# Batch 0 of a windowed attention and GEGLU kernel: v requested before the second run of q and k, the run's transposes placed behind the products with v

## Chip, cores, metric

One core of one Trainium2 chip. The metric is device time in microseconds (us). One execution that was traced gives the profile; each kernel was also run several times, and runs of the kernel before were taken on the same chip beside it. One run of the kernel before took 589 us; it is left out of everything below.

## The reference

```python
# q, k, v: (8 batches, 8 heads, 576 positions, 64)
scores = scale * q @ k^T + alibi bias;  mask: 0 <= i - j < 128
attn = softmax(scores);  o = attn @ v
x = o as (4608 tokens, 512)
out = (gelu(x @ w_gate) * (x @ w_val)) @ w_out      # d_ff = 1536
```

Operands on the chip are bf16, the output is f32.

## The kernel before

The kernel is one long stream of matmuls: attention of a batch runs ahead of the feed-forward part that uses it. The opening cannot do that: batch 0 needs its data first. Its first 320 positions (q and k as a "first run", five positions to a partition) are transposed, scored, exponentiated and masked, summed, multiplied with v, scaled into xT; then the first gate and value products start. The other 256 positions ("second run") are needed only for the scores after that. The stretch with the order before:

```python
load_runs(0, 0, 4, 8)            # first run, heads 4 to 7 (0 to 3 came earlier)
load_runs(0, 1, 0, 8)            # second run of q and k (kept in vb[1])
load_v(0, (0, 1, 2))
load_w(0, 256)
load_w(256, 640)
...
def rest(cs):                    # transposes of the second run, two head pairs at a time
    for w in (0, 1):             # q, k
        ps = bank().bitcast(BF16)
        for k, c in enumerate(cs):
            transpose_runs(0, 1, w, c, ps[:, 256 * k:256 * k + 256])
        untangle(act, 0, 1, w, slice(cs[0], cs[-1] + 1), ps)
...
keep_busy(8)                     # matmuls on zeros ahead of the next bank's first use
first((0, 1))                    # has keep_busy(3) between q and k
made_later()
keep_busy(4)
scores(0, 0, (0, 1), lambda: (keep_busy(3), first((2,)), first((3,))))
keep_busy(2)
scores(0, 0, (2, 3))
scores2(0)
keep_busy(4)
rest((0, 1))
keep_busy(1)
rest((2, 3))
sums0(0)
...
values_first((act, dve, act, dve))   # products with v, spread of 1/sum, scaling into xT
scores(0, 1, (0, 1), None, masks)
...                                  # gate_val: first gate and value products
```

`keep_busy(n)` puts n matmuls of 128x512 on zeros ahead of the next use of a PSUM bank, so that TensorE does not idle. In what follows these are "fillers".

The softmax here doesn't subtract the row's maximum and nothing guards it: scores larger than these inputs give would overflow.

Of the kernel before, what the change touches and what calls it, by code (L numbers as in the profile page):

```python
# [26 lines left out]
def kernel(  # L27
# [39 lines left out]
    def bank():  # L67
        ps = psum.tile([128, 512], FP32, name="ps")
        for _ in range(heat.pop()):
            nc.tensor.matmul(out=ps, lhsT=zeros[:, 0:128], rhs=zeros, start=True, stop=True)  # L70
        heat.append(0)
        return ps

    def keep_busy(n):
        heat[0] = n
# [20 lines left out]
    def load(t, src, b, js=range(5)):  # L96
        for j in js:
            lo = 64 if j == 0 else 0
            nc.gpsimd.dma_start(  # L99
                out=t[lo:128, j, :].rearrange("p (h d) -> p h d", h=H),  # L100
                in_=src[b][:, 128 * j - 64 + lo:128 * j + 64, :].rearrange("h p d -> p h d"))
# [10 lines left out]
    def runs(what, b, n):  # L112
        first, parts, r = RUNS[b][n]
        t, lo, p = (qs, ks)[what][b], 1536 * n, 0
        if (b, n) == (0, 1):

            t, lo = vb[1], 512 + 1024 * what
        elif b == 0:
            p = 64 * what
        return t.rearrange("p j x -> p (j x)")[p:p + parts, lo:lo + 512 * r].rearrange(  # L120
            "p (h x) -> p h x", h=H)

    def load_runs(b, n, h0, h1):
        first, parts, r = RUNS[b][n]
        for what, src in ((0, q), (1, k)):
            nc.gpsimd.dma_start(
                out=runs(what, b, n)[:, h0:h1, :],
                in_=src[b][h0:h1, first:first + parts * r, :].rearrange(
                    "h (p r) d -> p h (r d)", r=r))

    def load_v(b, js=range(5)):
        load(vb[b % 2], v, b, js)

    def load_w(lo, hi):
        for dst, src in ((wg, moe_w_gate), (wv, moe_w_val)):
            nc.gpsimd.dma_start(
                out=dst[:, :, lo:hi],
                in_=src[:, lo:hi].rearrange("(c p) f -> p c f", p=128))


    def by_pair(t):
        return t.rearrange("p j c t -> p (j c t)").rearrange("p (c x) -> p c x", c=4)

    def transpose_runs(b, n, what, c, ps):

        first, parts, r = RUNS[b][n]
        src = runs(what, b, n)
        p = 64 * what if (b, n) == (0, 0) else 0
        for x in range(r):
            for i in (0, 1):  # L150
                nc.tensor.transpose(  # L151
                    out=ps[64 * i:64 * i + 64, parts * x:parts * x + parts],
                    in_=src[:, 2 * c + i, 64 * x:64 * x + 64],
                    identity=ident[p:p + parts, p:p + parts])

    def untangle(copy, b, n, what, c, ps):

        first, parts, r = RUNS[b][n]
        dst = by_pair((qT, kT)[what][b])[:, c, 64 + first:64 + first + parts * r]
        if isinstance(c, int):  # L160
            copy(out=dst.rearrange("p (x r) -> p x r", r=r),  # L161
                 in_=ps[:, 0:parts * r].rearrange("p (r x) -> p x r", r=r))
        else:
            n = c.stop - c.start
            copy(out=dst.rearrange("p c (x r) -> p c x r", r=r),
                 in_=ps[:, 0:n * parts * r].rearrange("p (c r x) -> p c x r", c=n, r=r))
# [22 lines left out]
    def score(b, c, i, j, qj, n, ps, col):  # L189
        nc.tensor.matmul(  # L190
            out=ps[:, col:col + 128 * n].rearrange("p (n t) -> p n t", n=n),
            lhsT=blocks(kT, b, i, c, j, 1).rearrange("p n t -> p (n t)"),
            rhs=blocks(qT, b, i, c, qj, n),
            start=True, stop=True)

    def exp(dst, src):
        nc.scalar.activation(out=dst, in_=src, func=AF.Exp, scale=0.125)  # L197

    def mask(dst, m):
        nc.vector.tensor_tensor(out=dst, in0=dst, in1=m, op=ALU.mult)  # L200
# [17 lines left out]
    def scores(b, s, cs, then=None, later=None):  # L218


        pss = []
        for c in cs:
            ps = [bank(), bank()]
            pss.append(ps)
            for j, qj, n, col in (((0, 0, 2, 0), (1, 1, 2, 256)),
                                  ((4, 4, 1, 0), (2, 3, 1, 128), (3, 3, 2, 256)))[s]:
                for i in (0, 1):
                    score(b, c, i, j, qj, n, ps[i], col)
        if then:
            then()  # L230
        for c, ps in zip(cs, pss):
            P = p_pool[s].tile([128, 2, 512], BF16, name="P")
            probs[b, s, c] = P
            for i in (0, 1):
                exp(P[:, i, :], ps[i])
            args = (P.rearrange("p i (n x) -> p i n x", n=2),
                    emask[:, 2 * c:2 * c + 2, :].unsqueeze(2).to_broadcast((128, 2, 2, 256)))
            if later is None:
                mask(*args)
            else:  # L240
                later.append(args)
# [8 lines left out]
    def row(b):  # L250
        if b not in sumrow:
            sumrow[b] = r_pool.tile([128, S], FP32, name="r")
            recip[b] = r_pool.tile([128, 4, S], FP32, name="rb")
        return sumrow[b]
# [33 lines left out]
    def spread4_banks(b, s):  # L288
        lo, w = PART[s][0], WIDE[s]

        pss = [bank() for _ in range(4)]
        n = (4, 2)[s]
        for k in range(n):
            for g, ps in enumerate(pss):
                nc.tensor.matmul(  # L295
                    out=ps[:, w * k:w * k + w],
                    lhsT=sel[32 * g:32 * g + 32, 2 * k:2 * k + 2, :].rearrange("p i m -> p (i m)"),
                    rhs=row(b)[32 * g:32 * g + 32, lo:lo + w], start=True, stop=True,
                    tile_position=(32 * g, 0))
        return pss  # L300
# [48 lines left out]
    def products(b, s, cs):  # L349
        lo, hi = PART[s]  # L350
        pss = []
        for c in cs:
            ps = bank()
            pss.append(ps)
            for j, a, e in PIECES[s]:
                for i in (0, 1):
                    h = 2 * c + i
                    nc.tensor.matmul(  # L358
                        out=ps[64 * i:64 * i + 64, a:e],
                        lhsT=vb[b % 2][:, j, 64 * h:64 * h + 64],  # L360
                        rhs=prob(b, s, c, i, j, e - a),
                        start=(j == 2 * s), stop=(j == 2 * s + 2), skip_group_check=True)
        return pss
# [5 lines left out]
                out=xT[:, c, b * S + lo:b * S + hi], in0=ps[:, 0:hi - lo],  # L369
                in1=recip[b][:, c, lo:hi], op=ALU.mult)  # L370

    def values_first(copies):


        n, w = PART[0][1], WIDE[0]
        for c, ps in enumerate(products(0, 0, range(4))):
            copies[c](out=recip[0][:, c, 0:n], in_=ps[:, 0:n])
        for g, ps in enumerate(spread4_banks(0, 0)):
            nc.vector.tensor_tensor(  # L379
                out=xT[:, :, w * g:w * g + w], in0=recip[0][:, :, w * g:w * g + w],  # L380
                in1=ps[:, 0:4 * w].rearrange("p (c x) -> p c x", c=4), op=ALU.mult)
# [68 lines left out]
    for half, base, step, chan in ((0, 0, 1, -1), (1, -1, -1, 1)):  # L450
# [2 lines left out]
            out=t, in_=t, compare_op=ALU.is_ge, fill=1e9,  # L453
            base=base, pattern=[[step, 128]], channel_multiplier=chan)
    load_runs(0, 0, 4, 8)
    load_runs(0, 1, 0, 8)
    load_v(0, (0, 1, 2))
    load_w(0, 256)
    load_w(256, 640)
    load_v(0, (3, 4))  # L460
# [38 lines left out]
    act, dve = nc.scalar.copy, nc.vector.tensor_copy  # L499
    def first(cs):  # L500
        for w in (0, 1):
            if w and len(cs) == 2:
                keep_busy(3)
            for c in cs:
                ps = bank().bitcast(BF16)
                transpose_runs(0, 0, w, c, ps)
                untangle(dve, 0, 0, w, c, ps)

    def rest(cs):
        for w in (0, 1):  # L510
            ps = bank().bitcast(BF16)
            for k, c in enumerate(cs):
                transpose_runs(0, 1, w, c, ps[:, 256 * k:256 * k + 256])
            untangle(act, 0, 1, w, slice(cs[0], cs[-1] + 1), ps)

    keep_busy(8)
    first((0, 1))
    made_later()
    keep_busy(4)
    scores(0, 0, (0, 1), lambda: (keep_busy(3), first((2,)), first((3,))))  # L520
    keep_busy(2)
    scores(0, 0, (2, 3))
    scores2(0)
    keep_busy(4)
    rest((0, 1))
    keep_busy(1)
    rest((2, 3))
    sums0(0)
    masks, tails = [], []
    values_first((act, dve, act, dve))  # L530
    scores(0, 1, (0, 1), None, masks)
    scores(0, 1, (2, 3), None, masks)
    for f in range(4):
# [134 lines left out]
```

## Time and profile before

| | kernel before |
|---|---|
| time, median of the first 6 runs | 358.05 us (357.79 to 358.89) |
| the traced execution | 357.38 us |
| TensorE busy | 98% of the span |
| copies of c = 2 start on VectorE | 8.95 us |
| first gate product (L392) starts | 18.70 us |

The line numbers of the tables: L151 transposes, L190 scores, L197 exp, L200 mask, L282 sums, L358 products with v, L295 spread, L379 (L380 after) scaling into xT, L392 (L393 after) gate and value products, L70 fillers. The prediction below shows the chain of waits and the timelines.

### The profile page before, as it was taken

Reading aid. Unit: us, or ns where it says so; the run is one execution under the profiler, and the core shown is the slowest. Engines: PE = TensorE matmul, PEld = TensorE weight load, DVE = VectorE, ACT = ScalarE, POOL = GpSimd, SP = SyncE. Lnnn points to the kernel's source line nnn. Section 1 sums busy time; section 2 is a strip of 40 time slices with the busy share of each in tenths; the row PEclk is TensorE's granted clock in tenths of the full one; section 3 lists DMA queues with packets and bytes.
Section 4 is the critical chain, followed back from the end, with each engine's and each line's share of the span. In section 5 each row is a group of like instructions: output and inputs, shape, how many; then the busy total and the mean of one; then the engine's idle time right before and its main releaser. Section 6 shows DMA issues by size and latency. Waiting matters only on the chain.

```text
span 355.6 us, 7101 instructions
## 1 busy us (share of the span) xinstructions
PE 348.9 (98%) x2869; PEld 174.6 (49%) x2869; DVE 188.3 (53%) x327; ACT 185.8 (52%) x342; POOL 103.1 (29%) x137
## 2 busy tenths in 40 slices
PE   8999999999999999999999999999999999999996
PEld 3667545444454445445444545454444444444443
DVE  4876578344988646646455554655474404403320
ACT  5884495536877375633873297337832233313322
POOL 8943479500940275003900192004000000000000
PEclk9999999999999999999999999999999999999999
DMA  7999999999999099983997399859206020011002
GB/s 93 182 195 197 202 160 193 148 154 166 141 157 174 12 185 180 158 177 41 153 208 151 78 133 200 142 129 98 88 4 133 32 88 1 2 68 50 2 29 88
DMA packets 145632, 42.62 MB, mean 120 GB/s; under 512 B 131608, under 2 KB 138520, under 8 KB 145600
## 3 DMA queue, kind: packets, MB, share of 16 engines
q0 software_dynamic: 106368, 18.88, 69.5%
q1 hardware_dynamic: 36432, 17.31, 22.2%
q10 hardware_dynamic: 2800, 5.99, 7.8%
q8 instruction: 22, 0.36, 0.4%
q14 instruction: 10, 0.08, 0.1%
HBM read 43.65 MB, written 9.53 MB: 150 GB/s over the span
## 4 chain that ended last, share of the span: by engine, by line
PE 94%; DVE 4%; issue 0%; ACT 0%; ACTq 0%; DVEq 0%
PE ps L392 53%; PE ps L415 25%; PE ps L358 5%; PE ps L190 4%; PE ps L70 2%; PE ps L315 2%; DVE P L200 1%; DVE r L321 1%; PE ps L151 1%; PE ps L429 1%; DVE kT L161 1%; PE ps L295 1%; PE ps L282 0%; PE ps L341 0%; DVE xT L379 0%
## 5 line engine op out<-in xcount | busy, mean ns | idle before, releaser
L399 DVE TENSOR_TENSOR hT<-ps,gelu 128x512 bf16<-128x512 f32 (+2 forms) x115 | 73.7, 653 | 105.8 <-PE ps L392 90.8
L398 ACT ACTIVATE gelu<-ps 128x512 bf16<-128x512 f32 (+2 forms) x115 | 65.1, 571 | 115.3 <-PE ps L392 111.5
L392 PE MATMUL ps<-xT,wg 128*128 128x512 bf16 (+2 forms) x460 | 112.3, 367 | 0.2
L392 PE MATMUL ps<-xT,wv 128*128 128x512 bf16 (+2 forms) x460 | 112.1, 366 | 0.0
L415 PE MATMUL ps<-wo,hT 128*128 128x512 bf16 x420 | 95.7, 380 | 0.0
L197 ACT ACTIVATE P<-ps 128x512 bf16<-128x512 f32 x144 | 73.1, 631 | 7.0 <-PE ps L190 7.0
L392 PEld LDWEIGHTS <-wv 128*128 128x128 bf16 x460 | 44.6, 98 | 48.8
L392 PEld LDWEIGHTS <-wg 128*128 128x128 bf16 x460 | 43.2, 98 | 47.4 <-issue 0.5
L200 DVE TENSOR_TENSOR P<-P,emask 128x1024 bf16<-128x1024 bf16 (+1 forms) x79 | 49.1, 641 | 30.1 <-ACT P L197 29.7
L415 PEld LDWEIGHTS <-hT 128*128 128x128 bf16 x420 | 38.9, 98 | 47.9 <-issue 3.7
L99 POOL DMA_DIRECT2D vb<-in_v_dram x40 | 33.9, 887 | 13.0 <-DMA ks<-in_k_dram 6.5
L420 ACT COPY osb<-ps 128x512 f32<-128x512 f32 x31 | 18.6, 601 | 32.8 <-PE ps L415 32.8
L621 POOL COPY mark<-hT 1x2 bf16<-1x2 bf16 x4 | 0.7, 174 | 95.0 <-DVE hT L399 95.0
L368 DVE TENSOR_TENSOR xT<-ps,rb 128x256 bf16<-128x256 f32 (+1 forms) x60 | 22.9, 443 | 9.2 <-DMA rb<-rd 4.7
L321 DVE RECIPROCAL r<-ps 128x320 f32<-128x320 f32 (+1 forms) x14 | 26.6, 1931 | 1.3 <-PE ps L315 1.3
L99 POOL DMA_DIRECT2D qs<-in_q_dram x30 | 25.2, 862 | 7.2 <-DMA wo<-in_moe_w_out_dram 5.1
L99 POOL DMA_DIRECT2D ks<-in_k_dram x30 | 25.4, 899 | 2.8 <-DMA qs<-in_q_dram 2.6
L190 PE MATMUL ps<-qT,kT 64*128 64x256 bf16 (+1 forms) x384 | 22.3, 244 | 1.4 <-DVE kT L161 0.6
L190 PEld LDWEIGHTS <-kT 64*128 64x128 bf16 x384 | 13.4, 94 | 13.6 <-issue 9.5
L358 PE MATMUL ps<-P,vb 128*64 128x128 bf16 (+2 forms) x384 | 18.1, 244 | 0.0
L358 PEld LDWEIGHTS <-vb 128*64 128x64 bf16 x384 | 14.7, 110 | 5.2 <-issue 4.8
L70 PE MATMUL ps<-zeros 128*128 128x512 bf16 x25 | 8.3, 460 | 1.2 <-DVE zeros L440 1.2
(73 smaller groups left out, 117.4 us busy)
## 6 DMA issues: line engine op xcount, KB each, us to landing
out_dram<-osb SPq DMA_DIRECT2D x35, 256.0 KB, 3.9
rb<-rd ACTq DMA_DIRECT2D x10, 576.0 KB, 7.4
vb<-in_v_dram POOLq DMA_DIRECT2D x32, 128.0 KB, 7.3
qs<-in_q_dram POOLq DMA_DIRECT2D x24, 128.0 KB, 6.2
ks<-in_k_dram POOLq DMA_DIRECT2D x24, 128.0 KB, 6.6
wo<-in_moe_w_out_dram POOLq DMA_DIRECT2D x2, 768.0 KB, 18.3
wg<-in_moe_w_gate_dram POOLq DMA_DIRECT2D x2, 384.0 KB, 9.2
wv<-in_moe_w_val_dram POOLq DMA_DIRECT2D x2, 384.0 KB, 10.7
```

The lines of the kernel that those rows point to most:

```text
L99: nc.gpsimd.dma_start(out=t[lo:128, j, :].rearrange("p (h d) -> p h d", h=H), in_=src[b][:, 128 * j - 64 + lo:128 * j + 64, :].rearrange(" ...
L190: nc.tensor.matmul(out=ps[:, col:col + 128 * n].rearrange("p (n t) -> p n t", n=n), lhsT=blocks(kT, b, i, c, j, 1).rearrange("p n t -> p ( ...
L197: nc.scalar.activation(out=dst, in_=src, func=AF.Exp, scale=0.125)
L200: nc.vector.tensor_tensor(out=dst, in0=dst, in1=m, op=ALU.mult)
L321: nc.vector.reciprocal(row(b)[:, lo:hi], ps[:, 0:hi - lo])
L358: nc.tensor.matmul(out=ps[64 * i:64 * i + 64, a:e], lhsT=vb[b % 2][:, j, 64 * h:64 * h + 64], rhs=prob(b, s, c, i, j, e - a), start=(j == ...
L368: nc.vector.tensor_tensor(out=xT[:, c, b * S + lo:b * S + hi], in0=ps[:, 0:hi - lo], in1=recip[b][:, c, lo:hi], op=ALU.mult)
L392: nc.tensor.matmul(out=ps[:, 0:hi - lo], lhsT=w[:, c, 128 * f:128 * (f + 1)], rhs=xT[:, c, t0 + lo:t0 + hi], start=(c == 0), stop=(c == 3))
L398: nc.scalar.activation(out=gl[:, 0:hi - lo], in_=pg[:, 0:hi - lo], func=AF.Gelu)
L399: nc.vector.tensor_tensor(out=hid[g][:, f, lo:hi], in0=pv[:, 0:hi - lo], in1=gl[:, 0:hi - lo], op=ALU.mult)
L415: nc.tensor.matmul(out=po, lhsT=hid[g][:, f, 128 * t:128 * (t + 1)], rhs=wo[:, f, :], start=(f == 0), stop=(f == NF - 1))
L420: (nc.vector.tensor_copy if g < 2 and t < 2 else nc.scalar.copy)(out=osb, in_=po)
```

## The change

Intent: v is wanted before the second run if the second run's transposes stand behind the products; so request it first, take transposes and fillers from ahead of the sums, and split the copies between ScalarE and VectorE.

```diff
-    def values_first(copies):
+    def values_first(copies, then):
         for c, ps in enumerate(products(0, 0, range(4))):
             copies[c](out=recip[0][:, c, 0:n], in_=ps[:, 0:n])
+        then()
         for g, ps in enumerate(spread4_banks(0, 0)):
...
     load_runs(0, 0, 4, 8)
+    load_v(0, (0, 1, 2))
     load_runs(0, 1, 0, 8)
-    load_v(0, (0, 1, 2))
...
-                keep_busy(3)
+                keep_busy(2)
...
-            untangle(act, 0, 1, w, slice(cs[0], cs[-1] + 1), ps)
+            untangle((act, dve)[w], 0, 1, w, slice(cs[0], cs[-1] + 1), ps)
...
-    scores(0, 0, (0, 1), lambda: (keep_busy(3), first((2,)), first((3,))))
+    scores(0, 0, (0, 1), lambda: (keep_busy(2), first((2,)), first((3,))))
...
     keep_busy(4)
-    rest((0, 1))
-    keep_busy(1)
-    rest((2, 3))
     sums0(0)
...
-    values_first((act, dve, act, dve))
+    values_first((act, dve, act, dve), lambda: (rest((0, 1)), rest((2, 3))))
```

## The prediction

> **What bounds the kernel now.** I read the page first, then the chain of waits over the opening, then the timelines of VectorE and ScalarE from 10 us on, then the DMA issues one by one.
>
> ```profile
> PE 348.9 (98%) x2869; PEld 174.6 (49%) x2869; DVE 188.3 (53%) x327; ACT 185.8 (52%) x342; POOL 103.1 (29%) x137
> ...
> PE   8999999999999999999999999999999999999996
> ...
> PEclk9999999999999999999999999999999999999999
> ```
>
> TensorE is busy for 98% of the span, so it bounds the kernel nearly everywhere. The edit touches batch 0 only, which ends when the first gate products (L392) start at 18.70 us. After that TensorE has no idle gap until 57.79 us. So what the edit is worth is how far it moves 18.70: a shift there should be carried to the end one for one.
>
> The chain of waits, in order of time (start, length, what):
>
> ```profile
> 10.24 0.41 DVE kT L161
> 10.65 0.05 issue
> 10.69 0.62 PE ps L190 x12
> 11.31 0.97 PE ps L70 x4
> 12.28 0.57 PE ps L151 x16
> 12.85 0.32 PE ps L70
> 13.17 0.57 PE ps L151 x16
> 13.73 0.89 PE ps L282 x30
> 14.62 1.11 PE ps L358 x24
> 15.73 1.14 PE ps L295 x32
> 16.88 0.00 issue
> 16.88 0.90 DVE xT L379 x2
> ...
> 18.70 4.51 PE ps L392 x32
> ```
>
> L190 is scores, L70 idle-filling matmuls on zeros, L151 the transposes of the second run (the "rest"), L282 the sums, L358 products with v, L295 the spread of the reciprocals, L379 the scaling into xT that the gate products wait for. Between 11.31 and 13.73 TensorE does 1.14 us of transposes and 1.29 us of filling. Beside it, the other two engines (start, length):
>
> ```profile
> 10.32 3.04 ACT L197 ACTIVATE P<-ps 128x512 bf16<-128x512 f32 x6 [0.56 <-PE ps L190]
> ```
> ```profile
> 13.03 0.42 DVE L200 TENSOR_TENSOR P<-P,emask 128x512 bf16<-128x512 bf16 x1
> 13.40 0.42 DVE L200 TENSOR_TENSOR P<-P,emask 128x512 bf16<-128x512 bf16 x1
> 14.66 0.66 DVE L286 RECIPROCAL r<-ps 128x80 f32<-128x80 f32 x1 [0.83 <-PE ps L282]
> ```
>
> The reader should see a second chain: six exps on ScalarE run without a gap from 10.32 to 13.36, and the last mask on VectorE follows from 13.40 to 13.82. The sums start at 13.66 and take the last masked tile (P2) in their final 8 matmuls, about 14.4, so the masks are about 0.6 us ahead of them. The transposes thus lie in the shadow of exp and mask: moved away, they free little.
>
> **What the Trainium skill says.** "PSUM — Partial Sum Buffer", Engine vs sequencer instructions: matmuls start and complete in program order, and ScalarE and VectorE are strict FIFO. So when the sums wait for a mask, products and transposes behind them wait too. The trace agrees: no later matmul overtakes in 13.66 to 18.70. "TensorE: Matmul & The Clock Gate", What's actually happening: the array runs at half rate until busy for a window of about 3.4 us, and goes back after an idle window. The trace agrees on the first half: the opening 8 fillers are 0.43 us apart (1.60, 2.03, 2.46), later four of them take 0.97. "DMA: Bandwidth & Descriptors", Queues, rings and completion order: each DMA engine takes a ring's descriptors in order. The trace agrees, landings below follow the issues.
>
> **The change, part by part.**
>
> (a) Two of the fills lose one filler each: before the transposes of k for heads 0 to 3 (5.86 us), and before those of heads 4 to 7 (8.56). One filler is 0.97 / 4 = 0.24 us, so up to 0.48 goes. The data must have landed. The DMA issues (KB each, us to landing, start of issue from GpSimd's timeline):
>
> ```profile
> ks<-in_k_dram POOLq DMA_DIRECT2D x2, 160.0 KB, 3.5
> vb<-in_q_dram POOLq DMA_DIRECT2D x1, 256.0 KB, 5.5
> vb<-in_k_dram POOLq DMA_DIRECT2D x1, 256.0 KB, 6.0
> vb<-in_v_dram POOLq DMA_DIRECT2D x1, 128.0 KB, 5.8
> ```
>
> k of heads 0 to 3 is issued at 1.99 and lands at 5.49, needed at 5.62: fine. k of heads 4 to 7 is issued at 4.54 and lands at 8.04, needed at 8.56 - 0.48 = 8.08: just there. I take 0.45 us. The copies of c = 2, 3 on VectorE (8.95 to 10.63) start that much earlier, then scores, exps (ScalarE was idle for 0.56 before them, so they can move) and masks: last exp at 12.91, last mask at 13.82 - 0.45 = 13.37.
>
> (b) The 32 transposes and one filler leave the place ahead of the sums: 0.57 + 0.32 + 0.57 = 1.46 us. TensorE reaches the sums at 13.73 - 0.45 - 1.46 = 11.82, but the last mask ends at 13.37. After it come a hand-over of 0.05 (as from kT's copy, 10.65 to 10.69) and the last 8 of 72 matmuls (0.89 / 72 x 8 = 0.10): products start at 13.52 instead of 14.62 on the chain, or 14.55 in the timeline. I use the timeline's: 1.03 us sooner. Of the 0.45 + 1.46 = 1.91 us taken off TensorE, 0.88 turns into waiting for masks.
>
> (c) The transposes come back behind the products: 2 x 0.57 = 1.14 us, now on the path, since the spread follows in order. Products 13.52 to 14.63, transposes to 15.77, spread from 15.77. It started at 15.66. So the spread is 15.77 - 15.66 = 0.1 us later. The scaling started 1.22 us after the spread's start (16.88 - 15.66) and does so again, at 16.99. Its four instructions take 1.68, to 18.67, and L392, which came 0.14 after their end, starts at 18.81.
>
> (d) Copies. ScalarE keeps two of the four 128x512 copies (0.67 each), VectorE takes two. VectorE's 128x320 copies follow each other every 0.40, so 128x512 should take 0.40 x 512 / 320 = 0.64. VectorE: reciprocal 13.76 to 14.4, two copies of products of 0.49 to 15.4, the first copy of kT to 16.05, the second (its transposes end at about 15.97 with drain) to 16.7. It is free 0.3 us ahead of the scaling at 16.99. ScalarE has finished its exps by 12.91 and is no bound. The copies cost nothing on the path.
>
> (e) Order of the requests. v for blocks 0 to 2 is issued at 5.14 instead of 6.90, so it lands about 1.8 us sooner, near 12.5 at the latest, for use at 13.52. The second run is issued from 7.6 to 9.4, where v was. There the last v was issued at 8.45 and landed at 14.25; the second run's k, last of the same total of bytes, should land there too. Its q is needed at 14.63 and k at 14.9. Margin 0.4 to 0.6 us: no wait, by estimate.
>
> Sum at L392's first start: -0.45 (fillers) - 1.46 (moved and filler) + 0.88 (waiting for masks) + 1.14 (moved back), which is +0.11. Time: 358.08 + 0.1 = **358.2 us**.
>
> **The rivals.**
> 1. *TensorE does not wait for the masks*, and the three fillers are a plain gain: -0.7 us, 357.4. For it: the masks were not on the chain before. Against: they end only 0.6 us ahead of their use, and 1.46 us of work is taken from before it. I give it 15%.
> 2. *The second run lands late*: k has 256 KB in its last transfer, twice v's 128. If the queue isn't backlogged, the extra 128 KB at the 170 GB/s moved from 10 to 14 us take 0.75 us, landing at 15.0, a wait of 0.1 us; with contention from the weights behind it 0.5. The time would be 358.3 to 358.8. Against: about 0.5 MB is queued when the last issue ends (1472 KB asked for, 0.93 MB moved by 9.4 by the stretch table's rates), so order counts, not the size of the last piece. 25%.
> 3. *The clock falls back*, as TensorE now idles about 0.9 us among small matmuls with fewer fillers: half rate for some 3.4 us costs 1.7 us, 359.9. Against: the idle time is a quarter of a window, and four fillers stay. 4%.
> 4. *The k fill was really a wait for DMA*, so (a) gives only 0.2: everything 0.25 later, 358.45. For it: 8.04 against 8.08 is no margin. 20%.
>
> **Range and chances.** The centre is 358.2. The likely deviations are all under 1 us: rival 1 makes the low end, 357.4; rivals 2 and 4 together with the spread of the runs before (357.97 to 358.85) make the high end, 359.0. A change of 2% is 7.2 us, while all the work moved or removed is under 2.5 us, so faster and slower by 2% have only what I can't foresee: 0.01 each; within 2%: 0.98.
>
> **What would show it.** In the changed profile: the last mask ends near 13.4; the sums spread out with a wait for a mask just before their end; products start near 13.5; the transposes (L151 from vb) behind them with no wait for DMA; the spread near 15.8; scaling near 17.0; the first L392 near 18.8; no gap after. Wrong would be a wait for DMA before those transposes (rival 2), VectorE's copies of kT still running when the spread is done, filling matmuls 0.43 us apart after 5 us (rival 3), or a first L392 before 18.3 (rival 1).

## More of the kernel before

The traced execution was faster than all six of the kernel's own runs (357.38 against 357.79 to 358.89).

## The result, and the profile after

358.15 us median of 6 runs (357.80 to 360.22) against 358.05 (357.79 to 358.89): ratio 1.0006, 95% interval 0.9983 to 1.0029, the same. Ratios are the mean time of one kernel's runs over that of the other's in the same rounds, so not quite the ratio of the medians.

The traced execution of the changed kernel was its slowest, 360.22. Its chain of waits (start, length, what):

```profile
12.79 3.20 DVE P L200 x6
15.99 0.04 issue
16.04 0.32 PE ps L282 x6
16.36 1.11 PE ps L358 x24
17.46 0.05 PE ps L151
17.52 0.00 issue
17.52 1.05 PE ps L151 x31
18.57 0.88 PE ps L295 x25
19.45 0.26 issue
19.71 0.90 DVE xT L380 x2
...
21.54 4.51 PE ps L393 x32
```

The shape is the predicted one. The masks (L200) are on the chain, which they were not before; the sums end 0.37 after the last mask; the transposes follow the products; the scaling follows the spread. But everything is 2.6 to 2.8 us later than I had put it, because of something ahead of the masks. TensorE's timeline shows it, here the fillers of the kernel before:

```profile
6.30 1.04 PE L70 MATMUL ps<-zeros 128*128 128x512 bf16 x4
7.81 0.82 PE L70 MATMUL ps<-zeros 128*128 128x512 bf16 x3
```

and those of the changed kernel:

```profile
7.44 1.49 PE L70 MATMUL ps<-zeros 128*128 128x512 bf16 x3 [0.34 <-issue]
9.83 0.96 PE L70 MATMUL ps<-zeros 128*128 128x512 bf16 x2
```

Two fillers take about as long as four did. (The `x3` at 7.44 is a group of four of which the trace lacks one record.) In the kernel before, TensorE's array came to full rate at about 4.6 us; in this execution it was at half rate until about 10.6 us, 9.4 us after its first matmul. Up to the second early filler the two kernels' TensorE programs are the same: 8 fillers, 20 transposes, 2 fillers. So this one trace cannot be laid beside the other.

### The profile page after: what moved, and what is told of

The parts are those of the page before. It is cut to its first block, busy times and chain, and to the rows that moved or that the text cites. A ratio compares the mean times of both kernels' runs of the same rounds, so it can differ in the third digit from the quotient of the medians.

```text
span 358.4 us, 7050 instructions
## 1 busy us (share of the span) xinstructions
PE 348.4 (97%) x2823; PEld 175.5 (49%) x2866; DVE 190.2 (53%) x329; ACT 185.1 (52%) x340; POOL 103.1 (29%) x137
## 3 DMA queue, kind: packets, MB, share of 16 engines
HBM read 43.65 MB, written 9.53 MB: 148 GB/s over the span
## 4 chain that ended last, share of the span: by engine, by line
PE 92%; DVE 5%; issue 1%; ACT 0%; ACTq 0%; DVEq 0%
PE ps L393 52%; PE ps L416 24%; PE ps L358 5%; PE ps L190 4%; DVE P L200 2%; PE ps L315 2%; PE ps L70 2%; DVE r L321 1%; PE ps L151 1%; PE ps L430 1%; DVE kT L161 1%; PE ps L295 0%; PE ps L341 0%; PE ps L282 0%; DVE xT L380 0%
## 5 line engine op out<-in xcount | busy, mean ns | idle before, releaser
L393 PE MATMUL ps<-xT,wg 128*128 128x512 bf16 (+2 forms) x444 | 110.4, 366 | 0.9
L416 PE MATMUL ps<-wo,hT 128*128 128x512 bf16 x401 | 94.3, 380 | 1.1 <-issue 0.2
L200 DVE TENSOR_TENSOR P<-P,emask 128x1024 bf16<-128x1024 bf16 (+1 forms) x79 | 49.2, 641 | 30.4 <-ACT P L197 29.9
```

The source lines that it names most:

```text
L200: nc.vector.tensor_tensor(out=dst, in0=dst, in1=m, op=ALU.mult)
L393: nc.tensor.matmul(out=ps[:, 0:hi - lo], lhsT=w[:, c, 128 * f:128 * (f + 1)], rhs=xT[:, c, t0 + lo:t0 + hi], start=(c == 0), stop=(c == 3))
L416: nc.tensor.matmul(out=po, lhsT=hid[g][:, f, 128 * t:128 * (t + 1)], rhs=wo[:, f, :], start=(f == 0), stop=(f == NF - 1))
```

## The experiments

Eleven runs, with the kernel before beside them. First a table that all of the accounts below use. "Full rate" is the start of the first clock record in the trace file (`0/clock` of trace.npz). No view prints it: the views count the time ahead of that record as full and show a granted clock of 1.00 throughout; the spacing of fillers and transposes agrees with the record. "Copies" is the start of VectorE's copies of c = 2, "gate" the start of the first gate product, "rest" the time of the traced execution less "gate".

| kernel (early fillers) | full rate | copies | gate | gate - copies | time | rest |
|---|---|---|---|---|---|---|
| before (3, 3) | 4.57 | 8.95 | 18.70 | 9.75 | 357.38 | 338.68 |
| e9, before again (3, 3) | 5.03 | 9.11 | 19.08 | 9.97 | 357.76 | 338.68 |
| e2, fillers only (2, 2) | 5.73 | 8.95 | 18.82 | 9.87 | 357.49 | 338.67 |
| e8, more fillers out (2, 2) | 5.32 | 8.81 | 18.96 | 10.15 | 357.65 | 338.69 |
| e3, move only (3, 3) | 4.86 | 9.04 | 19.25 | 10.21 | 358.06 | 338.81 |
| e1, changed again (2, 2) | 6.02 | 9.09 | 19.30 | 10.21 | 358.42 | 339.12 |
| e7, weights cut at 384 (2, 2) | 6.58 | 9.31 | 19.53 | 10.22 | 358.21 | 338.68 |
| e10, changed, third (2, 2) | 5.80 | 8.98 | 19.73 | 10.75 | 358.44 | 338.71 |
| changed (2, 2) | 10.59 | 11.11 | 21.54 | 10.43 | 360.22 | 338.68 |
| e5, requests as before (2, 2) | 10.38 | 11.00 | 21.27 | 10.27 | 360.00 | 338.73 |
| e6, copies on ScalarE (2, 2) | 10.39 | 11.01 | 21.56 | 10.55 | 360.24 | 338.68 |
| e11, cold start (2, 2) | 11.43 | 11.17 | 21.86 | 10.69 | 360.55 | 338.69 |
| e4, requests only (3, 3) | 7.05 | 9.97 | 21.99 | 12.02 | 360.67 | 338.68 |

The last column is the check on the prediction's first step: in eleven of thirteen traces the time is 338.67 to 338.73 us after the first gate product. A shift there is carried to the end one for one.

### e1_after_again: the changed kernel again

No edit.

> The changed kernel unaltered, for a second trace and more times: in the first trace TensorE stayed at half rate (fillers 0.43 us apart) until about 10.7 us, in the kernel before only until about 4.7. Theory A (masks hide the moved transposes): with an early warm-up the last mask ends near 13.4, products start near 13.6 to 13.7, the transposes behind them wait for no DMA, first gate product at 18.8 to 19.0, time 358.2. Rival B (second run lands late; k landed at 8.44 + 7.1 = 15.54 in the first trace, where the late warm-up hid it): TensorE waits for DMA at about 15.5 and the first gate product is at 19.3 to 19.6, time 358.6 to 358.9. Theory C on the clock: the warm-up at 10.7 was chance[...], so this trace shows either; rival D: fewer fillers make it late always, and this trace shows fillers 0.43 us apart up to 10 us again.

Measured: 358.09 us (357.48 to 358.50), ratio 0.9990 (0.9976 to 1.0005). This time full rate came at about 6 us. TensorE's timeline (start, length, what, idle time before):

```profile
13.30 1.03 PE L282 MATMUL ps<-P,ones 128*32 128x80 bf16 x30 [0.35 <-DVE P L200]
14.27 1.18 PE L358 MATMUL ps<-P,vb 128*64 128x192 bf16 x24
15.28 1.06 PE L151 MATMUL ps<-ident,vb 128*64 128x128 bf16 x32
16.27 1.13 PE L295 MATMUL ps<-r,sel 32*128 32x80 f32 x32
...
19.30 0.70 PE L393 MATMUL ps<-xT,wg 128*128 128x320 bf16 x4
...
22.41 0.72 PE L393 MATMUL ps<-xT,wv 128*128 128x320 bf16 x4 [0.23 <-DMA wv<-in_moe_w_val_dram]
```

The sums wait for a mask (first line), and there is no wait for DMA at the transposes: theory A's path, later than its 18.8 to 19.0 for the first gate product. New is the last line. The third value tile waits for the second request of wv; in the kernel before it started 2.72 us after the first gate product, here 3.11. That 0.39 is nearly all of what this trace has above 338.68 in the last column (0.44). It was in none of my rivals. The DMA issues show why it can wait. This request is issued at 11.5 to 11.6 us in both kernels; in the kernel before it took

```profile
wv<-in_moe_w_val_dram POOLq DMA_DIRECT2D x1, 384.0 KB, 9.3
```

and in e1

```profile
wv<-in_moe_w_val_dram POOLq DMA_DIRECT2D x1, 384.0 KB, 10.7
```

Over all traces with the weights cut at 256 it landed at 20.8 to 21.6 with v requested last (before, e2, e5, e8, e9) and at 21.7 to 22.5 with v first (changed, e1, e3, e4, e6, e10, e11). From 8 to 11 us the DMA moved 155 and 159 GB/s in e2 and e8, and 134 and 123 in the changed kernel and e1. Why it moves less is not tested; v's requests bring 64 or 128 KB for 0.7 to 0.9 us of GpSimd's issuing, the second run's 256 KB for 0.9. The packets differ too: under 512 bytes, 1856 of them moved in these 3 us in e2, and 2533 in e1.

### e2_fills_only: only the three fillers go

```diff
-                keep_busy(3)
+                keep_busy(2)
...
-    scores(0, 0, (0, 1), lambda: (keep_busy(3), first((2,)), first((3,))))
+    scores(0, 0, (0, 1), lambda: (keep_busy(2), first((2,)), first((3,))))
...
     rest((0, 1))
-    keep_busy(1)
     rest((2, 3))
```

> The kernel before with only the three fillers taken out (two ahead of transposes of the first run, one between the transposes of the second), nothing moved, requests as before. Theory A: the fillers were on the path, and with the transposes still ahead of the sums the masks stay hidden: last mask at 13.4, products at 13.78 instead of 14.55, first gate product at 17.93, so -0.77 us, 357.3 against 358.05, faster than both kernels. Rival: the fillers only filled waits for data (k of heads 4 to 7 lands at 8.04), then at most -0.5. Rival D: fewer fillers delay the warm-up of the array, and it is slower than the kernel before by up to 2 us in many runs.

Measured: 357.71 us (357.49 to 357.97) against 358.27, ratio 0.9981 (0.9967 to 0.9994): 0.68 us off, as theory A had it (0.77), and the interval excludes no change. The time came out; the trace's first gate product did not (18.82, not 17.93): full rate came at about 5.7 us there instead of 4.6, and the sums paused for 0.3 us up to 14.37, after the last mask had ended at 13.82. The profile names no releaser for that pause. So where the gain in the times arises is not shown by this trace alone; part (a) of the section on the prediction comes back to it.

### e3_move_only: the fillers come back

```diff
-                keep_busy(2)
+                keep_busy(3)
...
-    scores(0, 0, (0, 1), lambda: (keep_busy(2), first((2,)), first((3,))))
+    scores(0, 0, (0, 1), lambda: (keep_busy(3), first((2,)), first((3,))))
```

(on the changed kernel)

> The changed kernel with the two early fillers put back (3 and 3 as before): order of requests, place and copies of the transposes as changed. Theory A: all of scores, exps and masks are 0.45 us later than in the changed kernel, and since the masks end the wait ahead of the sums, so is the first gate product, at 19.3; time 358.6, +0.5 on the kernel before: the move by itself costs half a microsecond that the fillers gave back. Rival: the fillers lie in the wait for the masks, and it equals the changed kernel, 358.15.

Measured: 358.19 us (357.87 to 358.89), ratio 0.9997 (0.9983 to 1.0012). A miss for the time: +0.5 is outside the interval, if not by much. The trace says 19.25 for the first gate product, as expected, and 10.21 from the copies to it against 9.75 and 9.97 in the two traces of the kernel before. So the move costs 0.24 to 0.46 on the path of this trace; but what it makes of the times is lost in their spread (0.4 to 0.6 from one run to the next). Nor do the times show a loss from the two fillers put back: 358.19 here, 358.09 to 358.15 for the changed kernel.

### e4_order_only: only the requests change places

```diff
     load_runs(0, 0, 4, 8)
+    load_v(0, (0, 1, 2))
     load_runs(0, 1, 0, 8)
-    load_v(0, (0, 1, 2))
```

(on the kernel before)

> The kernel before with only the two request lines exchanged (v ahead of the second run), transposes still ahead of the sums. If the second run's k lands at 15.5 (first trace of the changed kernel), TensorE waits for DMA ahead of or within the transposes from about 12.2 to 15.5, and the first gate product moves from 18.7 to about 21.4: 360.8, +2.7. If it lands near 14.3, as my prediction had it, +1.5. If the order of requests does not matter, 358.05.

Measured: 361.25 us, ratio 1.0085 (1.0066 to 1.0104), +3.0 us. The chain of waits:

```profile
8.44 7.24 DMA vb<-in_k_dram
15.68 0.04 issue
15.72 0.41 PE ps L151 x8
```

The second run's k lands at 15.68, as in the first trace of the changed kernel and not at 14.25, where I had predicted it. With the transposes ahead of the sums, TensorE waits for it. So v can be requested first only if the transposes move too.

### e5_old_order: the move without the requests

```diff
     load_runs(0, 0, 4, 8)
-    load_v(0, (0, 1, 2))
     load_runs(0, 1, 0, 8)
+    load_v(0, (0, 1, 2))
```

(on the changed kernel)

> The changed kernel with the two request lines back as before (second run ahead of v); place and copies of the transposes and fillers as changed. In traces with v last, v's third block lands at 14.25 to 14.9; the products start at about 14.3 and want that block about 0.2 us later. Theory A: TensorE waits 0 to 0.4 us for v in the products, but the weights of the second request (wv, columns 256 to 640), which landed at 22.0 to 22.4 in every trace with v first and at 20.8 to 21.3 with v last, come a microsecond sooner and are waited for no more; time 358.1, level with the changed kernel within 0.3. Rival: the request order is what the move needs, and without it TensorE waits for v by more than half a microsecond: 358.7 or more.

Measured: 359.38 us (357.86 to 360.09), ratio 1.0018 (0.9995 to 1.0041). Three of six runs were near 360, and the traced one shows half rate until past 10 us, so the products started at 16.18, long after v's last block (14.37). Whether TensorE would wait for v in a quick start stays open. By estimate it would, by some tenths: in the five traces with v last that block landed at 14.2 to 15.0, and the products of the changed kernel started at 14.2 to 14.3 in its two quick starts. wv landed at 21.55 and was not waited for.

### e6_act_copies: the copies stay on ScalarE

```diff
-            untangle((act, dve)[w], 0, 1, w, slice(cs[0], cs[-1] + 1), ps)
+            untangle(act, 0, 1, w, slice(cs[0], cs[-1] + 1), ps)
```

(on the changed kernel)

> The changed kernel with all four copies of the second run on ScalarE, as before. Theory A: ScalarE is free from 15.7 us on (early warm-up) and takes one each 0.48 us, so the fourth is done at 17.8, ahead of the scores of c = 2 that need it at 18.4; the scaling is unhindered; equal to the changed kernel, 358.1 within 0.2. Rival: the split of the copies is worth something, because exp of the scores follows on ScalarE: 0.3 us slower.

Measured: 358.69 us (357.68 to 360.24), ratio 1.0006 (0.9982 to 1.0031). Again a late start in the trace and in two of six runs; the median is no evidence. In the trace VectorE idles for 1.82 us ahead of the scaling, and what ends that is the spread, not a copy. The split is worth nothing that these runs can see. The transposes took 1.38 us here, 1.06 to 1.28 in the undisturbed ones elsewhere. The difference is a pause up to 17.53, after the first of them; the first copy starts at 17.95, so the copies do not make it. I have no explanation for it.

### e7_w384: more weights in the first request

```diff
-    load_w(0, 256)
-    load_w(256, 640)
+    load_w(0, 384)
+    load_w(384, 640)
```

(on the changed kernel)

> The changed kernel with the first two weight requests cut at column 384 instead of 256, so that the third gate and value tiles come with the first request. Theory A (v first starves the queue, the weights land a microsecond later and the third value tile waits 0.1 to 0.3 us for wv): the wait is gone, 357.9, 0.1 to 0.3 us under the changed kernel. The larger first request lands about 1 us later, at about 18.9, still ahead of its use at 19.3 to 19.8; where that fails, the first gate product waits and it is no faster. Rival: the wait was a chance of one trace: equal.

Measured: 358.09 us (357.82 to 358.37), ratio 0.9986 (0.9970 to 1.0003). No wait for wv in the trace. The median is e1's; a gain of 0.1 to 0.3 is smaller than the noise. The wait in e1 was real, but e10, too, waited hardly at all, its gate being late itself: it costs something only in the quick starts (e1, and 0.1 in e3).

### e8_fills_zero: four more fillers out of e2

```diff
     scores2(0)
-    keep_busy(4)
     rest((0, 1))
     rest((2, 3))
```

(on e2)

> The fillers-only kernel (transposes ahead of the sums) with the four fillers ahead of those transposes taken out too. Theory A: the last mask, not TensorE, sets when the sums end; TensorE does 0.97 us less ahead of them and waits 0.97 us longer for the mask. Products start 0.3 to 0.4 us after the last mask's end, time 357.7, equal to the fillers-only kernel within 0.2. Rival: TensorE's own work still set it: 357.0 to 357.3. Rival D: with TensorE less busy the array falls back to half rate, and it is slower by 1 us or more.

Measured: 357.64 us (357.55 to 358.44), ratio 0.9979 (0.9963 to 0.9994). Equal to e2, as expected, but not for the reason that I gave. TensorE's timeline:

```profile
12.34 0.86 PE L151 MATMUL ps<-ident,vb 128*64 128x128 bf16 x24 [0.83 <-DMA vb<-in_k_dram]
```

and the weight loads', which run beside the matmuls:

```profile
15.00 0.77 PEld L358 LDWEIGHTS <-vb 128*64 128x64 bf16 x20 [0.32 <-DMA vb<-in_v_dram]
```

Without the fillers TensorE waits for the second run's k and, later, for v's last block. In the kernel before, those four fillers lay in the shadow of a transfer as well as of the masks. The opening is tight against three things at once: masks, second run, v.

### e9_before_again: the kernel before again

No edit.

> The kernel before, unaltered, for a second trace. Theory: in ten traces the time was 338.68 us plus the start of the first gate product, plus any wait for weights after it, and the start of the copies of c = 2 (8.8 to 11.1 us) moved with the moment at which the array came to full rate. So here too time = 338.7 + first gate product within 0.1, and from the copies of c = 2 to the first gate product it is 9.75 as in the first trace, whenever the warm-up comes; median of its runs 358.0 to 358.6, with the first trace's 357.4 at the lucky end. Rival: the 9.75 of the first trace was luck too, and it is 10.0 to 10.2, so that the move of the transposes costs nothing.

Measured: 358.15 us (357.49 to 358.79), ratio 0.9998 (0.9984 to 1.0012). 338.68 + 19.08 is the time of its traced execution, 357.76. From copies to gate it took 9.97, between the theory (9.75) and the rival (10.0 to 10.2): the sums had a pause near their end (sums start to products 1.11, in the first trace 0.89). So 9.75 was a good draw, by 0.2.

### e10_after_third: the changed kernel, third trace

No edit.

> The changed kernel, unaltered, for a third trace, on the same chip as the kernel before. Theory: 10.2 to 10.45 from the copies of c = 2 to the first gate product, weights' second wv request landing after 21.8. Times: mostly 357.5 to 358.7; if fewer early fillers let the array stay at half rate until past 10 us in some runs (six of 42 runs of kernels with the two fewer were over 359.5 us, none of 34 with all of them), one or two of six near 360. Rival: the runs near 360 belong to two or three loads by chance, and none here.

Measured: 358.15 us (357.49 to 358.44), ratio 0.9995 (0.9982 to 1.0007). No run near 360. From copies to gate 10.75, outside the expected range, and TensorE's timeline says why:

```profile
15.91 0.86 PE L151 MATMUL ps<-ident,vb 128*64 128x128 bf16 x24 [0.35 <-DMA vb<-in_k_dram]
```

k of the second run landed at 15.87 (issued at 8.46, 7.4 us). This is the prediction's rival 2, in one of three traces.

### e11_cold_start: no fillers while the first data come

```diff
-    keep_busy(8)
     first((0, 1))
```

(on the changed kernel)

> The changed kernel without the eight fillers that run while the first data are on their way. Theory (the spread of times comes from when the array reaches full rate): TensorE starts cold at 4.7 us in every run, stays at half rate until 8 to 11 us, fillers 0.43 us apart up to then, copies of c = 2 at 10 to 11.2 us, and the time is 359.0 to 360.3 in every run. Rival: the late traces have another cause, and it is 358.1 like the changed kernel.

Measured: 359.86 us (359.06 to 360.55), ratio 1.0040 (1.0027 to 1.0054). All six runs over 359, as the theory had it (one, 360.55, above its 360.3). TensorE's timeline:

```profile
6.90 1.89 PE L70 MATMUL ps<-zeros 128*128 128x512 bf16 x4
...
21.86 0.70 PE L393 MATMUL ps<-xT,wg 128*128 128x320 bf16 x4
```

Four fillers in 1.89 us, half rate. Full rate came at 11.43, the copies of c = 2 at 11.17. So a late arrival at full rate is by itself enough for the 2 us that the first trace of the changed kernel had lost.

## Why the prediction was right, by its steps

**The bound.** Right, and exactly: see the table's last column. 338.68 is also what the first trace gives (357.38 - 18.70).

**(a) Fillers, -0.45.** Right in size, once the moment of full rate is allowed for. The copies of c = 2 start at 8.81 to 9.31 with two fillers in the five quick starts, at 8.95 to 9.11 with three, and at 9.97 in e4: no gain to see, because the moment of full rate moves them as much. The prediction had taken that moment from one trace and held it fixed. At the same moment the kernels do differ. On the line through e9 (5.03, 9.11) and e4 (7.05, 9.97), which also passes within 0.04 of the two other traces with three fillers, the copies would start at 9.23, 9.41, 9.44, 9.53 and 9.77 at the moments of e8, e2, e10, e1 and e7; they start 0.42 to 0.46 earlier. This is an estimate; the times alone show less: 0.68 us by the ratio for all three fillers in e2 (0.77 expected), and nothing clear for the two in e3.

The Trainium skill ("TensorE: Matmul & The Clock Gate", What's actually happening) calls the activity window free-running, so that the kernel's start may fall anywhere in it. The traces agree: full rate came at 4.57 and 5.03 in two traces of the kernel before, at 6.02, 5.80 and 10.59 in three of the changed one, and the full-rate records last 351.57 us in nine traces and 348.16 in four, one step of 3.41 us apart. Such a start can account for a spread of one step, not for the 10.59; see "What stays open". My rival 3 looked for a fall back to half rate. Its sign, fillers 0.43 us apart after 5 us, did show in the first trace of the changed kernel (7.44 and 7.87), but there full rate had not come yet; a fall back showed in no trace. The danger was a late start.

Rival 4 rested on a reading that was slightly off: 8.04 for the landing of k of heads 4 to 7 used the median delay of two requests; this one landed at 8.09, just after the 8.08 at which it was to be wanted. No trace shows a wait for it.

**(b) 0.88 of waiting for masks.** Right. From copies to products the prediction has 13.52 - 8.50 = 5.02, and all three traces of the changed kernel have 5.18; the kernel before had 5.60 and 5.82. The 0.16 over is the last 8 matmuls of the sums behind the last mask, which take about 0.26 and not 0.10. I had divided the time of all 72 by 72.

**(c) 1.14 for the transposes on the path.** Right in two traces of three: from the products' start to the spread's the prediction has 2.25, the traces 2.00, 2.21 and, with the wait for k, 2.54. From the spread to the gate 3.04 was predicted and 3.03 to 3.04 found.

**(d) Copies free.** Right: in every changed trace they were done before the scaling, which waited for the spread.

**(e) Requests.** This step failed. k was to land at 14.25, as the last of the same bytes. The landings did follow the issues in all thirteen traces, but the same bytes in another order did not take the same time: k landed at 14.5 to 15.9 in the eight traces with v first, and the weights behind it came about a microsecond later than before. In the quick starts of the changed kernel that costs 0.35 (e10, at k) or 0.4 (e1, at wv); in its late one it is hidden. So the margin of 0.4 to 0.6 us that the prediction gave k was no margin. Its rival 2 had the landing (15.0) and the wait (0.1 to 0.5) better, though its reason, the size of the last piece, is not tested.

**The sum.** From copies to gate 10.31 was predicted and 10.21, 10.43 and 10.75 found, against 9.75 and 9.97 before: the move costs 0.24 to 1.0 us, about 0.6 on the mean of three against the mean of two. The fillers gave about 0.45 back, by the estimate under (a). All the runs of either kernel as it stands give means of 358.34 (44 runs of before) and 358.19 (18 of the changed one), with deviations of 0.47 and 0.62 from run to run: no difference that I could call one, and the predicted +0.1 is well inside. By the times alone, any forecast of no change would have been as right; what speaks for this one is that its parts are found in the traces. How the gain and the loss divide to within 0.3 us the times cannot say (e3 missed).

**Where the expected gain went.** The transposes had stood in the shadow of exp and mask (and, as e8 shows, their fillers in that of a transfer), so moving them away freed TensorE only to wait; put behind the products they were on the path.

**What stays open.** Whether fewer early fillers make late starts more frequent: 6 of 47 runs of kernels with two and two fillers and the eight in front were over 359.5 us, none of the 50 of before and e3; but five of the six fell in two kernels of one call. The clock records point that way without settling it. Their lengths suggest that full rate comes only in steps of 3.41 us. Then the late starts missed a moment one step earlier: in the changed kernel, e5 and e6 at 7.18, 6.97 and 6.98 us. e4, with three early fillers, came to full rate at 7.05. Up to there the TensorE programs differ only in the third filler, at 6.2 us. That is one trace against three, and no run was made for it. Open is also the pause in the sums in e2, e8 and e9, for which the profile names nobody.

**A better version.** e2 and e8, with v last, the transposes where they were, and the fillers thinned: 0.19 and 0.21% under the kernel before. Neither comes near 2%.

## What to carry to other kernels

Work in the shadow of another engine costs nothing where it is; before moving it, ask what the freed engine will wait for, and whether its new place is on the path. Changing the order of requests in a queue with a backlog can move everything queued behind (here the weights, by about 1 us), not only the two that change places. And where the runs of one kernel differ by 1 to 2 us, take two traces of each kernel and compare stretches between marks inside them: one trace of each would have shown here a loss of 2.8 us that isn't one.

## What the Trainium skill lacked or had wrong

- "TensorE: Matmul & The Clock Gate": it tells to get past the first busy window of about 3.4 us of matmuls. Here full rate came 9.4 us after the first matmul in the first trace of the changed kernel, and 3.4 us after it in the first trace of the kernel before, by the same program up to the tenth filler. The page gives no figure for an opening in which fillers and transposes alternate.
- "DMA: Bandwidth & Descriptors": its fit for one DMA from GpSimd (2.0 us plus bytes over 436 GB/s) makes an estimate of 2.4 us for the 160 KB of the first run; the traces have 3.2 to 4.1 us, for these first requests (160 KB each, thirteen traces). That the order of differently cut requests delays all behind them is on no page: wv landed at 20.8 to 21.6 with v last, 21.7 to 22.5 with v first.
